# Attention followed by a SwiGLU block on one core: the first block's third chunk is projected with the third block's in a wide group, the output weights are asked for later, the last visits are dealt anew

## The chip, the core and the metric

The kernel runs on one core of a Trainium2 chip. The core has a matrix engine (TensorE, PE in the profile; its weight loads are listed as PEld), a vector engine (VectorE, DVE), an activation engine (ScalarE, ACT), GpSimd (POOL) and a queue engine (SyncE, SP). TensorE writes its products into PSUM, here eight banks of 512 single-precision columns on 128 partitions. Vector and activation engine read them from there. Transfers between the chip's memory and the core's are issued by POOL and SP and carried out by 16 DMA engines that both share. The metric is the device time of one execution in microseconds; lower is better.

## The reference

Twelve heads of softmax attention over eight batches of 448 tokens, head size 64, then a gated feed-forward layer (768 to 1536 and back) over all 3584 tokens:

```python
scores = scale * np.matmul(q, k.transpose(0, 1, 3, 2))
attn = exp(scores - max) / sum
x = (attn @ v).transpose(0, 2, 1, 3).reshape(B * S, H * D)   # 3584 x 768
g = x @ w_gate                                              # 768 x 1536
silu = g * (1.0 / (1.0 + np.exp(-g)))
val = x @ w_val
out = silu * val @ w_out                                    # 1536 x 768
```

## The kernel before

**Attention in pairs, units and visits.** Two heads make a pair; there are 48 pairs, six to a batch. From pair 12 on (`QUAD`), the scores of two neighbouring pairs are made in seven units: three key chunks of each pair and one unit that holds the remaining keys of both (`RU`). A unit (`qk_quad`, L349 to L383) is a few matmuls into one PSUM tile of pool `ps_s` (three buffers of two banks), and one exponential of 128 x 896 on ACT (L378) into SBUF. When all units of a pair are there, 32 or 40 small matmuls (L462, "PV" below) multiply the exponentials with the values. They write into two tiles `acc`, one for each head, of pool `ps_f`, which has two buffers of one bank. DVE closes each tile with a reciprocal (L504) and a multiplication (L505).

The program is written out by hand as a row of visits, and each engine works its own instructions in the order of the program. A visit of the middle and late part starts three units, runs the PV of at most one pair whose units all belong to earlier visits (some visits have none), and then takes some feed-forward work. `VISITS` (L1100) deals that work to the visits from `base` on: a row says which block begins, how many gate-and-value steps run (`nf`), how many wide groups (`ng`), how many plain outputs (`no`), and how many vector sums (`ns`). Visits are numbered here from `base`, the row's index in `VISITS`; the ones before `base` have negative numbers, and there `run_budget` spreads the work over the visits by its time.

**Where operands come from.** POOL loads the pairs' queries, keys and values (L203, L180), the weights (`load_w`, L223) and copies each pair's queries and keys into an order that suits a transposing transfer (L240). SP issues this transfer (`qkT<-qk`, L244), and only then can the pair's units start. `wq` (L1043) says behind which pair the weights and some further loads are asked for. POOL works its loads and copies in program order, and every load goes through one queue.

**The feed-forward blocks.** Two batches make 896 tokens, cut into a block of 384 and one of 512 tokens. Blocks 0 to 3 (batches 0 to 3) run during attention, in 12 gate-and-value steps each, whose results stand in `hts`. The output projection is made for chunks of 128 tokens in two ways:

- Plain: `plain_out` (L724), 12 matmuls into one PSUM tile for 384 output columns (`OH`) or 192 (`QW`).
- In a wide group: `OutPair.wide` (L807) makes two chunks together by seven products of six 384-column matmuls (L759), a Strassen-like scheme, with sums of the chunks made beforehand on DVE (`h_sums`) and combinations on DVE and ACT between the products. It takes one `ps_s` tile and one `ps_f` tile.

Before the change the three chunks of block 0 and the third chunk of block 2 are plain, the first in six halves at visits -11 to -8 and the last in four quarters at visits 25, 26, 27 and 29. The five wide groups of this stage stand at visits 5, 8, 20, 28 and 31. `run_group` takes a list `behind` of units: for a visit with a group and no PV, the visit's three units are not started ahead of the group but two inside it and the third after it.

**After attention.** The last four batches are projected in `Unit`s (L897), again by seven products instead of eight, 448 columns wide. A unit's second PSUM bank is first written by ACT and then added to by matmuls. For the first two units of each half a matmul with the identity (`Z`, L964) writes that bank beforehand, so that later matmuls add to what ACT writes. Four such matmuls run in all. Outputs are collected in `osb` tiles of pool `fp` (four buffers) and stored by SP.

Of the kernel before, what the change touches and what calls it, by code (L numbers as in the profile page):

```python
# [10 lines left out]
FP32 = mybir.dt.float32  # L11
FP16 = mybir.dt.float16
# [5 lines left out]
NB = 2  # L18
# [3 lines left out]
LA = 6  # L22
# [43 lines left out]
def kernel(  # L66
# [87 lines left out]

    wo_all = consts.tile([128, 2, NFB, OH], FP16, name="wo")
    wo = [wo_all[:, i] for i in range(2)]
    qk16s = [consts.tile([128, 2, NC, 2, D], FP16, name=f"qk16_{i}") for i in range(3)]

    raw = {}
# [6 lines left out]
            nc.tensor.matmul(wp[:, 0 : w * 128], lhsT=warm[:], rhs=warm4[:, 0:w], start=True, stop=True)  # L166

    def load_qk32(pr):
        rq = fp.tile([P, 2, NC, D], FP32, tag="osb", bufs=4, name="rq")
        rk = fp.tile([P, 2, NC, D], FP32, tag="osb", bufs=4, name="rk")  # L170
        for dst, src in ((rq, q), (rk, k)):
            nc.sync.dma_start(dst[:], src[0, 2 * pr : 2 * pr + 2].rearrange("h (p c) d -> p h (c d)", c=NC))
        raw[pr] = (rq[:], rk[:])
# [570 lines left out]
            store(osb, kk, c0 + ch * 128, 128, 0, DM)  # L744

    def new_osb():
        return fp.tile([128, DM], FP32, tag="osb", bufs=4, name="osb")

    def ffn2_steps(kk, c0, hts, steps):
        osbs = {}  # L750
# [146 lines left out]
    class Unit:  # L897


        def __init__(self, u, w, x, tsum, hts):  # L900
            self.u, self.hts, self.w = u, hts, w
            self.kind = "gv"[u % 2]
            self.x, self.tsum = x, tsum
            self.g = ps_s.tile([128, 2, 512], FP32, tag="s", name="un")
            self.a, self.e = self.g[:, 0, 0:w], self.g[:, 1, 0:w]
            self.by = {"a": [], "e": []}
# [56 lines left out]

        def Z(self):  # L964
            self.bank()
            nc.tensor.matmul(self.b, lhsT=ident[:], rhs=self.xb(0, 0)[:, 0], start=True, stop=True)

        def A1(self):
            if self.u > 1:
# [48 lines left out]
    with tc.manual_schedule():  # L1018
# [6 lines left out]
        for vo in Vts:  # L1025
# [19 lines left out]
            1: [("V", 2), ("qk", 8, 1), ("g", 1), ("v", 1)],  # L1045
            3: [("qk", 9, 1), ("qk", 10), ("g", 2), ("v", 2)],
            4: [("g", 3), ("v", 3), ("qk", 12)],
            6: [("V", 3), ("o", 0)],
            8: [("o", 1)],
        }  # L1050

        def emit(item):
# [18 lines left out]
        def add_block(i, visits):  # L1071
            if i < B - 2 * NB:
                f1, own, n = block(i)
                fvq.extend(f1)
                kk, c0, hts = own
            else:
                own = None
            t_out = NFB * OH / 2400.0
            if i == 0:
                oq.extend([(ffn2_steps(*own, by_half(range(n // 128), OH)), t_out)] * (2 * (n // 128)))  # L1080
            if i < 2:
                if i:
                    ffn2_wait.append(own)
                    sums.extend(wsums)
                    wsums.clear()
                return
            kk, c0, hts = ffn2_wait.pop()
            ffn2_wait.append(own)
            odd = i % 2 == 0
            new = [OutPair(kk, c0, hts, t, 1 - t if i == B - 2 * NB else t) for t in range(1 + odd)]  # L1090
            groups.extend(new)
            if not odd:
                w = QW
                oq.extend([(ffn2_steps(kk, c0, hts, by_half([2], w)), t_out)] * (DM // w))
            for pair in new:
                pair.todo = pair.sums()
                sums.extend(pair.todo)
# [10 lines left out]
        ]  # L1108

        def token_sums(x, w, t, eng=nc.vector):  # L1110
# [61 lines left out]

        def run_group(units):
            pair = groups.pop(0)
            if units:
                sums.insert(0, lambda: None)
                sums.insert(1, tsums6.pop(0))
            assert not any(f in sums for f in pair.todo)
            keep = [fp.tile([128, 512], FP32, tag=tag, name=name) for tag, name in (("sg", "p1"), ("t1", "p15"))]
            pair.wide(keep, add_sum, (1, 1, 0), units[:2])  # L1180
            for unit in units[2:]:
                qk(*unit)
# [93 lines left out]
        for x, (chunks, todo) in enumerate(plan):  # L1276
# [12 lines left out]
            lone = nf == 1 and bool(todo)  # L1289
            behind = []  # L1290
            for n, (pr, c) in enumerate(ordered if x else []):
                if ng and not todo:
                    behind.append((pr, c, small))
                    continue
                if n == 2 and ordered[n] in quads:
                    rests = open_products(rests, small)
                late = n == 2 and not todo and c < NC and pr < QUAD and bool(fvq) and not fvq[0].at[1]
                late = late or n == 2 and lone and not fvq[0].at[1]
                qk(pr, c, small, late)
# [15 lines left out]
            for pr in entered:  # L1315
                lead = [pr + 3] if pr + 3 < QUAD else [pr + 3, pr + 4] if pr + 3 == QUAD else [pr + 4]
                for p in lead:
                    if NPE <= p < NPAIR and p not in QPE:
                        ready.append(prep(p))
                if 14 <= pr + LA < NPAIR:  # L1320
                    load_qk16(pr + LA, 1)
                if 12 <= pr + 3 < NPAIR:
                    load_v(pr + 3)
# [77 lines left out]
                tsums6.pop(0)()  # L1401
            for u in {len(VISITS) + base - 6: range(2), len(VISITS) + base - 2: range(2, 3)}.get(x, []):
                weight_sums(u)
            while held and not fvq:
                turn_x(held.pop(0))
            while turns:
# [52 lines left out]

        def units_of(kk, t, last):  # L1460
            units = {}
            items = unit_items(units, lambda u: Unit(u, S, X[kk], t, hts), S)
            pairs = [OutPair(kk, 0, hts, p, p % 2, last and p == 2) for p in range(3)]
            if last:
                mixed = OutPair(kk, 0, hts, 0, 1)
                mixed.x, mixed.y = apart_chunk, hts[:, :, ts(6, 128)]
                mixed.rows = [(kk - 1, 6 * 128), (kk, 6 * 128)]
                pairs.insert(1, mixed)
                pairs[2].at = 2
            for n in range(NH):  # L1470
                after = [f"G{n - 1}"] if n else [f"F00_{NH - 1}", f"F10_{NH - 1}", f"D1_{NFB - 1}"]
                items[f"G{n}"] = (PE_, OH / 2400 + 0.0025, after, lambda n=n: pairs[0].begin(n))
            items["H0"] = (DVE_, 0.65, [f"F00_{NH - 1}", f"F10_{NH - 1}"], pairs[0].sums()[0])
            for part, f0, n, u in (("e", 0, 4, NFB - 3), ("l", 4, 2, NFB - 1)):
                for m, fn in enumerate(pairs[0].sums(f0, n)[1:], 1):
                    after = [f"F00_{u}", f"F10_{u}", "H0"] + [f"H{m - 1}{part}"] * (m > 1)
                    items[f"H{m}{part}"] = (DVE_, 0.07 + 0.1 * n, after, fn)
            return items, pairs
# [70 lines left out]
```

## Time and profile before

| | |
|---|---|
| median of three runs | 419.72 us (419.65 to 419.94) |
| the profiled execution's own time | 420.16 us |
| its span, first to last instruction | 418.4 us |
| mean granted TensorE clock | 1.000 |
| PE busy | 412.3 us, 4346 matmuls |
| DVE busy | 271.1 us |
| ACT busy | 248.9 us |
| POOL busy | 227.5 us |

Times within the span are given from its start. A row of the timeline has start, duration, engine, line, operation, tile, shape and count, and in brackets how long the engine was idle before and what ended that. A duration of several merged matmuls includes the last one's way through the array, so neighbouring rows overlap; the distance from start to start is what a row takes of the engine. A row of the windows view has the stretch, its length, each engine's busy time with its count of instructions, the granted clock, the busy share of the DMA engines (several transfers at once can take it over 1) and what they moved in GB/s.

### The profile page before, as it was taken

The numbers are of one execution on the slowest core, as the hardware profiler recorded it, in microseconds if no ns is written. First come the engines' busy times: TensorE is split into PE (matmuls) and PEld (weight loads), VectorE is DVE, ScalarE is ACT, GpSimd is POOL, SyncE is SP. The second block draws the span as 40 slices with busy tenths as digits, with TensorE's granted clock in tenths as the row PEclk, the third lists the DMA queues.
The fourth block names the chain that finished last, engine by engine and source line by source line (L and its number), as shares of the span: only waits on it lengthen the run. The fifth ranks groups of instructions, "written<-read, shape, count | busy, mean of one in ns | idle before, by whom it ended". The sixth has DMA issues, their size and how long they took to land.

```text
span 418.4 us, 10870 instructions
## 1 busy us (share of the span) xinstructions
PE 412.3 (99%) x4346; PEld 260.6 (62%) x4346; DVE 271.1 (65%) x630; ACT 248.9 (59%) x387; POOL 227.5 (54%) x346
## 2 busy tenths in 40 slices
PE   8999999999999999999999999999999999999996
PEld 3666666555577776787767676555555555555654
DVE  4767562566786774677756577765757665757763
ACT  6985676666577665787657686655453345454121
POOL 8856533999998983599977815599700000000000
PEclk9999999999999999999999999999999999999999
DMA  8999999999999999999999944600000430000225
GB/s 135 180 199 200 200 177 195 137 169 206 197 167 140 151 207 146 183 153 160 157 153 183 107 59 105 190 14 0 2 0 2 129 99 0 2 0 0 76 80 149
DMA packets 108196, 50.29 MB, mean 120 GB/s; under 512 B 60401, under 2 KB 104817, under 8 KB 108145
## 3 DMA queue, kind: packets, MB, share of 16 engines
q0 software_dynamic: 46848, 24.56, 51.4%
q1 hardware_dynamic: 61024, 24.79, 32.9%
q8 instruction: 34, 0.56, 0.6%
q10 hardware_dynamic: 272, 0.25, 0.2%
q14 instruction: 18, 0.14, 0.1%
HBM read 49.55 MB, written 11.01 MB: 145 GB/s over the span
## 4 chain that ended last, share of the span: by engine, by line
PE 81%; DMA 13%; POOL 4%; issue 1%; ACT 0%; DVE 0%; POOLq 0%
PE un L929 13%; PE gp L610 11%; PE og L759 11%; PE ub L929 10%; PE vp L610 9%; PE acc L462 9%; PE ob L759 8%; PE s L356 5%; DMA wv<-in_moe_w_val_dram 5%; DMA qkraw<-in_q_dram 4%; DMA wg<-in_moe_w_gate_dram 2%; DMA qkT<-qk 2%; PE op L732 2%; POOL qkraw L203 2%; PE s L368 1%
## 5 line engine op out<-in xcount | busy, mean ns | idle before, releaser
L378 ACT ACTIVATE E<-s 128x896 f16<-128x896 f32 x126 | 107.4, 916 | 37.5 <-PE s L356 27.4
L610 PE MATMUL gp<-X,wg 128*128 128x256 f16 (+3 forms) x402 | 61.7, 300 | 0.0
L610 PE MATMUL vp<-X,wv 128*128 128x256 f16 (+3 forms) x402 | 58.6, 289 | 0.0
L240 POOL COPY qk<-qkraw 128x512 f16<-128x512 f16 x70 | 44.8, 681 | 22.8 <-DMA qkT<-qk 21.9
L610 PEld LDWEIGHTS <-wv 128*128 128x128 f16 x444 | 41.7, 98 | 14.5
L180 POOL DMA_DIRECT2D vraw<-in_v_dram x72 | 43.8, 624 | 11.4 <-DMA wo<-in_moe_w_out_dram 7.6
L180 POOL DMA_DIRECT2D qkraw<-in_k_dram x70 | 42.3, 616 | 6.9 <-DMA wo<-in_moe_w_out_dram 3.9
L610 PEld LDWEIGHTS <-wg 128*128 128x128 f16 x402 | 35.5, 98 | 15.8 <-issue 2.2
L403 ACT ACTIVATE E<-s 112x896 f16<-112x896 f32 x48 | 40.7, 918 | 7.5 <-PE s L393 7.5
L462 PEld LDWEIGHTS <-E 128*128 128x128 f16 (+2 forms) x1224 | 38.1, 98 | 8.4 <-issue 3.1
L462 PE MATMUL acc<-vo,E 128*128 128x65 f16 (+2 forms) x1224 | 42.0, 193 | 0.1
L759 PEld LDWEIGHTS <-hts 128*128 128x128 f16 x282 | 27.1, 98 | 17.0
L690 DVE SCALAR_TENSOR_TENSOR t<-sg,gp 128x384 f32<-128x384 f32 (+1 forms) x29 | 17.4, 614 | 25.6 <-ACT sg L637 25.6
L696 DVE SCALAR_TENSOR_TENSOR hts<-t,vp 128x256 f16<-128x256 f32 (+3 forms) x67 | 30.9, 461 | 3.4 <-PE vp L610 1.2
L505 DVE TENSOR_TENSOR xt<-acc,R 128x256 f16<-128x256 f32 x72 | 30.6, 425 | 2.5
L203 POOL DMA_DIRECT2D qkraw<-in_q_dram x44 | 29.9, 679 | 3.2 <-PE tp L324 1.0
L356 PE MATMUL s<-qkT 64*64 64x448 f16 (+1 forms) x288 | 28.7, 352 | 0.3 <-DMA qkT<-qk 0.3
L994 ACT ACTIVATE silu<-un 128x448 f32<-128x448 f32 x24 | 13.1, 544 | 21.7 <-PE un L929 21.1
L759 PE MATMUL og<-wo,hts 128*128 128x384 f16 x132 | 25.4, 326 | 0.0
L978 DVE TENSOR_TENSOR un<-ub,kept 128x448 f32<-128x448 f32 x24 | 15.1, 630 | 15.5 <-ACT kept L975 9.8
L982 DVE TENSOR_TENSOR kept<-ub,kept 128x448 f32<-128x448 f32 x24 | 15.0, 625 | 13.3 <-PE ub L929 13.3
L971 ACT ACTIVATE ub<-un 128x448 f32<-128x448 f32 x24 | 12.7, 529 | 15.5 <-PE un L929 13.9
(213 smaller groups left out, 746.6 us busy)
## 6 DMA issues: line engine op xcount, KB each, us to landing
vraw<-in_v_dram POOLq DMA_DIRECT2D x72, 64.0 KB, 5.2
qkraw<-in_q_dram POOLq DMA_DIRECT2D x41, 112.0 KB, 4.8
qkraw<-in_k_dram POOLq DMA_DIRECT2D x68, 64.0 KB, 4.9
out_dram<-osb SPq DMA_DIRECT2D x7, 336.0 KB, 3.2
wg<-in_moe_w_gate_dram POOLq DMA_DIRECT2D x8, 288.0 KB, 9.4
wv<-in_moe_w_val_dram POOLq DMA_DIRECT2D x8, 288.0 KB, 10.0
wo<-in_moe_w_out_dram POOLq DMA_DIRECT2D x2, 1152.0 KB, 18.8
out_dram<-osb SPq DMA_DIRECT2D x7, 288.0 KB, 3.7
```

What stands on the lines that cost most here:

```text
L180: eng.dma_start(dst[ts(s, 64)], rows)
L203: nc.gpsimd.dma_start(dst, flat.rearrange("h (p c) d -> p h (c d)", c=NC))
L240: nc.gpsimd.tensor_copy(dst.rearrange("p c h d -> p h c d"), src)
L356: nc.tensor.matmul(s[ts(half, m), hx, 0:S].rearrange("p (c q) -> p c q", q=P), lhsT=t[ts(hx, 64), ds((c + low(pr, hx)) * 128 + half * m, m ...
L378: nc.scalar.activation(e, s[:, :, 0:S], AF.Exp, scale=sm_scale)
L403: nc.scalar.activation(e[:, :, 0:S], s[0:P, :, 0:S], AF.Exp, scale=sm_scale)
L462: nc.tensor.matmul(acc[ds(lo, m), ts((j + pr % 2) % (KR + 1), D + 1)], lhsT=e[rows, ds(hx * S + j * 128 + lo, m)], rhs=Vts[pr % NV][rows, ...
L505: nc.vector.tensor_tensor(xt[:, :, hx], a4[:, :, 0:D], r[:].unsqueeze(2).to_broadcast([128, KR + 1, D]), ALU.mult,)
L610: nc.tensor.matmul(dst[:, 0:w], lhsT=wslice(kind, self.fb, cb), rhs=X[kk][:, cb, ds(c0 + lo, w)], start=(cb == 0), stop=(cb == NCB - 1),)
L696: nc.vector.scalar_tensor_tensor(self.hts[:, self.fb, ds(lo, w)], self.t1[:, ds(lo, w)], 0.5 * HS, vp[:, 0:w], ALU.mult, ALU.mult)
L759: nc.tensor.matmul(dst, lhsT=lhs(n), rhs=rhs(n), start=first and n == 0, stop=n == NH - 1, skip_group_check=True)
L929: mm = nc.tensor.matmul(dst, lhsT=lhs[:, n], rhs=rhs[:, n], start=first and n == 0, stop=n == NK - 1, skip_group_check=True,)
```

## The change

Block 0's third chunk is no longer projected plainly. Two DVE copies at x = 14 and 16 (visits -5 and -3) keep its 128 tokens in a new tile `first_single`. When block 3 is added, a group `mixed` is built of that chunk and block 2's third chunk, which replaces the four quarters. So six plain halves become four, four plain quarters go, and there are six wide groups instead of five. `osb` gives up one of its four buffers, which makes room for `first_single`.

`wq` asks for the two halves of `w_out` behind pairs 8 and 9 instead of 6 and 8, and pair 15's queries and keys behind the second half. POOL's order around it becomes: third group of values, pair 11's copies, pair 14's load, first half of `w_out`, pair 13's copies, pair 12's values, second half of `w_out`, pair 15's load, pair 14's copies. Before, the first half of `w_out` stood ahead of pair 11's copies, the second ahead of pair 13's, and pair 12's values behind pair 15's load.

The last visits are dealt anew: visit 24 has one gate-and-value step and visit 25 the last one (before: two at visit 24, none at 25). The wide groups stand at 20, 27, 29 and 31, and nothing but attention stands at 26, 28, 30 and 32. For a group in a visit behind such an empty one, the visit's units now also go into and behind the group where the visit has a PV. PE's order from visit 25 on is then, with U for a unit: 3 U, PV 40, a step in halves | 3 U, PV 41 | PV 42, group with 2 U inside, 1 U | 3 U, PV 43 | PV 44, group with 2 U inside, 1 U | 3 U, PV 45 | group with 2 U inside, 1 U | 1 U, PV 46, PV 47. Before it was: 3 U, PV 40, quarter | 3 U, PV 41, quarter | 3 U, PV 42, quarter | 3 U, PV 43, group | 3 U, PV 44, quarter | 3 U, PV 45 | group with 2 U inside, 1 U | 1 U, PV 46, PV 47.

`Z` writes only the columns that no earlier matmul has written into that bank: 188 of 448 in the first half, 64 in the second, without clearing.

```diff
+    first_single = consts.tile([128, NFB, 128], FP16, name="single")
...
-        rq = fp.tile([P, 2, NC, D], FP32, tag="osb", bufs=4, name="rq")
+        rq = fp.tile([P, 2, NC, D], FP32, tag="osb", bufs=3, name="rq")
...
         def Z(self):
             self.bank()
-            nc.tensor.matmul(self.b, lhsT=ident[:], rhs=self.xb(0, 0)[:, 0], start=True, stop=True)
+            lo = self.primed
+            nc.tensor.matmul(
+                self.b[:, lo:],
+                lhsT=ident[:],
+                rhs=self.xb(0, 0)[:, 0, lo:],
+                start=False,
+                stop=True,
+                skip_group_check=True,
+            )
...
-            6: [("V", 3), ("o", 0)],
-            8: [("o", 1)],
+            6: [("V", 3)],
+            8: [("o", 0)],
+            9: [("o", 1), ("qk", 15, 1)],
...
-                oq.extend([(ffn2_steps(*own, by_half(range(n // 128), OH)), t_out)] * (2 * (n // 128)))
+                oq.extend([(ffn2_steps(*own, by_half(range(2), OH)), t_out)] * 4)
...
-            new = [OutPair(kk, c0, hts, t, 1 - t if i == B - 2 * NB else t) for t in range(1 + odd)]
+            new = [OutPair(kk, c0, hts, t) for t in range(1 + odd)]
             groups.extend(new)
             if not odd:
-                w = QW
-                oq.extend([(ffn2_steps(kk, c0, hts, by_half([2], w)), t_out)] * (DM // w))
+                mixed = OutPair(kk, c0, hts, 0, 1)
+                mixed.x, mixed.y = first_single, hts[:, :, ts(2, 128)]
+                mixed.rows = [(0, 2 * 128), (kk, c0 + 2 * 128)]
+                new.append(mixed)
+                groups.append(mixed)
...
-            (0, 0, 1, 0, 0), (0, 1, 0, 0, 0), (0, 1, 0, 0, 0), (0, 1, 0, 0, 0), (0, 2, 0, 0, 0),
-            (4, 0, 0, 1, 1), (0, 0, 0, 1, 1), (0, 0, 0, 1, 2), (0, 0, 1, 0, 0), (0, 0, 0, 1, 2),
-            (0, 0, 0, 0, 0), (0, 0, 1, 0, 0), (0, 0, 0, 0, 0),
+            (0, 0, 1, 0, 0), (0, 1, 0, 0, 0), (0, 1, 0, 0, 0), (0, 1, 0, 0, 0), (0, 1, 0, 0, 0),
+            (0, 1, 0, 0, 0), (4, 0, 0, 0, 1), (0, 0, 1, 0, 1), (0, 0, 0, 0, 2), (0, 0, 1, 0, 1),
+            (0, 0, 0, 0, 2), (0, 0, 1, 0, 0), (0, 0, 0, 0, 0),
...
         def run_group(units):
             pair = groups.pop(0)
-            if units:
+            if units and not groups:
                 sums.insert(0, lambda: None)
                 sums.insert(1, tsums6.pop(0))
...
-                if ng and not todo:
+                if ng and (not todo or not any(VISITS[x - base - 1][1:4])):
                     behind.append((pr, c, small))
                     continue
...
-                if 14 <= pr + LA < NPAIR:
+                if 14 <= pr + LA < NPAIR and pr + LA != 15:
                     load_qk16(pr + LA, 1)
...
+            if x in (14, 16):
+                part = ds((x - 14) // 2 * NH, NH)
+                nc.vector.tensor_copy(first_single[:, part], hview(0, 384)[:, part, ts(2, 128)])
```

More of the change, by code (lines that the diff above doesn't have):

```diff
@@ L746, in new_osb @@
     def new_osb():
-        return fp.tile([128, DM], FP32, tag="osb", bufs=4, name="osb")
+        return fp.tile([128, DM], FP32, tag="osb", bufs=3, name="osb")
     def ffn2_steps(kk, c0, hts, steps):
@@ L897, with __init__ @@
     class Unit:
[L900 to L901 removed]
+        def __init__(self, u, w, x, tsum, hts, primed):
+            self.u, self.hts, self.w, self.primed = u, hts, w, primed
             self.kind = "gv"[u % 2]
@@ L1461, in units_of @@
             units = {}
-            items = unit_items(units, lambda u: Unit(u, S, X[kk], t, hts), S)
+            items = unit_items(units, lambda u: Unit(u, S, X[kk], t, hts, OH if last else (KR + 1) * (D + 1)), S)
             pairs = [OutPair(kk, 0, hts, p, p % 2, last and p == 2) for p in range(3)]
```

2 lines of the change are left out of this document (1 added, 1 removed).

## The prediction

> **What bounds the kernel now.** I read the page first, then TensorE's waits, then the stages that the change touches: windows, timeline, POOL's queue.
>
> ```profile
> span 418.4 us, 10870 instructions
> PE 412.3 (99%) x4346; PEld 260.6 (62%) x4346; DVE 271.1 (65%) x630; ACT 248.9 (59%) x387; POOL 227.5 (54%) x346
> DMA  8999999999999999999999944600000430000225
> PE s L356 <- DMA qkT<-qk: 0.3, 1, 0.3
> ```
>
> PE is the bound, and its longest wait for data is 0.3 us (last line, from the waits by engine). So every matmul removed is time won, unless it lets PE run into something that it now just misses. The DMA row shows a candidate: the DMA engines are full until the 23rd slice.
>
> The last visits of attention, by windows: visits 24 and 25; 26 and 27; 28; 29 and 30; 31; the end up to the first `Unit`.
>
> ```profile
> 232.71:241.32 8.61, 8.61 (x93) 5.25 (x92) 4.94 (x13) 5.84 (x8) 7.24 (x11) 1.00 0.80 96
> 241.32:248.58 7.26, 7.26 (x168) 5.81 (x167) 5.73 (x18) 6.89 (x10) 0.76 (x1) 1.00 0.26 51
> 248.58:255.50 6.92, 6.92 (x48) 4.01 (x46) 3.67 (x10) 2.70 (x5) 2.14 (x2) 1.00 0.68 91
> 255.50:259.93 4.43, 4.43 (x90) 3.36 (x90) 4.10 (x11) 3.75 (x5) 1.96 (x3) 1.00 0.43 86
> 259.93:267.45 7.52, 7.52 (x56) 4.07 (x52) 4.95 (x10) 4.41 (x7) 4.35 (x5) 1.00 0.74 190
> 267.45:270.22 2.77, 2.75 (x71) 2.12 (x71) 2.51 (x7) 2.25 (x3) 1.42 (x2) 1.00 0.76 217
> sum 37.51, PE 37.49 PEld 24.62 DVE 25.90 ACT 25.84 POOL 17.88; mean PE 6.25 PEld 4.10 DVE 4.32 ACT 4.31 POOL 2.98
> ```
>
> In visits 26 and 27 ACT (fourth busy column, 6.89 of 7.26 us) is nearly as full as PE: the exponentials are close to being the bound there, and a quarter of plain output is what PE does meanwhile. A group without units takes 6.92 us, one with two units inside 7.52.
>
> **The last visits.** The change takes the four quarters out and puts a sixth group in. What it also does is to set PV 41 against PV 42 and PV 43 against PV 44 with nothing between. Each PV takes both `ps_f` banks.
>
> ```profile
> 244.82 1.14 PE L462 MATMUL acc<-vo,E 64*128 64x65 f16 x32
> 245.80 1.15 PE L732 MATMUL op<-wo,hts 128*128 128x192 f16 x12
> 246.40 0.42 DVE L505 TENSOR_TENSOR xt<-acc,R 128x256 f16<-128x256 f32 x1
> 246.88 0.38 PE L368 MATMUL s<-qkT 64*64 64x448 f16 x4
> 255.50 0.74 PE L356 MATMUL s<-qkT 64*128 64x448 f16 x6
> 255.96 2.54 ACT L378 ACTIVATE E<-s 128x896 f16<-128x896 f32 x3 [0.84 <-PE s L356]
> 256.08 1.25 PE L462 MATMUL acc<-vo,E 64*128 64x65 f16 x32
> 256.28 0.85 DVE L1114 TENSOR_TENSOR vraw<-X 128x1344 f16<-128x1344 f16 x1
> L378 ACT ACTIVATE E<-s 128x896 f16<-128x896 f32 x126 | 107.4, 916 | 37.5 <-PE s L356 27.4
> ```
>
> A PV holds PE for 0.98 us (244.82 to 245.80), but DVE has read its second bank only at 246.82 (246.40 + 0.42), 2.0 us after the PV began. Before, the quarter (1.08 us, 245.80 to 246.88) and the next units filled that time. Now PE waits: 2.0 + 0.05 - 1.0 = 1.05 us, twice. Behind the waiting PV stand, on PE, its own matmuls and the whole group.
>
> The second wait is for `ps_s`. Behind the groups at 27 and 29 stand one unit and then the next visit's three: four units in a row with three tiles, so the fourth waits for the first's exponential. Three units take PE 0.58 us (255.50 to 256.08); an exponential starts 0.46 us behind its unit (255.96) and takes 0.916. So the fourth starts at 0.46 + 0.92 + 0.03 = 1.4 us instead of 0.6: 0.8 us, at visits 28 and 30. These units' exponentials follow at (2.54 - 0.92) / 2 = 0.81 us and end 3.8 us behind the group; PV 44 wants the last at about 4.0, so ACT doesn't add to it.
>
> Stretch by stretch, from the same point as the windows:
> - Visits 24 and 25: the same two steps, less one quarter: 8.61 - 1.08 = 7.5 us.
> - 26 and 27: units 0.58, PV 41 to PV 42 2.05, PV 42 1.0, group with two units of 0.19 and their change of shape 7.4: 11.0.
> - 28 and 29: units 1.6, PV 43 to PV 44 2.05, PV 44 1.0, group 7.4: 12.05.
> - 30: units 1.6, PV 45 1.0: 2.6. Then 7.52 + 2.77 = 10.3 as before.
>
> Together 43.5 us against 37.51: **+6.0**. Without the four waits (2 x 1.05 + 2 x 0.8 = 3.7) it would be +2.3, the lower bound; the upper is one us more, if DVE's sums, which now stand between the closes of the two PVs (the largest 0.85 us, 256.28), also come late.
>
> ```profile
> 238.80 2.48 SPq L550 DMA_TRANSPOSE X<-xt  x2
> 241.33 1.23 SPq L556 DMA_TRANSPOSE X<-xt  x1
> ```
>
> On SP, the transposes of pairs 36 to 40, held until the last step is done, now start at visit 25's end. PV 42's closing needs the third of them gone (issued 2.5 us behind the first). That close comes 3.5 us into visit 26, so DVE may stand there for an estimated 1 to 2 us; but PE needs the bank next for the group's third product, two products (6.92 / 7 each) and two units behind PV 42, 2.4 us. I count nothing.
>
> **The first block.** Four plain halves instead of six.
>
> ```profile
> L732 PE MATMUL op<-wo,hts x72: 323/326/337, 64.8 to 81.8; 128*128 128x384 f16 x72
> 48.80 16.49 DMA qkraw<-in_q_dram
> 56.26 0.59 POOL L180 DMA_DIRECT2D qkraw<-in_k_dram  x1 [0.74 <-DMA vraw<-in_v_dram]
> 64.44 0.59 POOL L180 DMA_DIRECT2D vraw<-in_v_dram  x1 [7.59 <-DMA wo<-in_moe_w_out_dram]
> 72.44 0.59 POOL L180 DMA_DIRECT2D qkraw<-in_k_dram  x1 [3.92 <-DMA wo<-in_moe_w_out_dram]
> 67.36 9.11 DMA qkT<-qk
> 74.56 1.18 POOL L240 COPY qk<-qkraw 128x512 f16<-128x512 f16 x2
> L244 SPq DMA_TRANSPOSE qkT<-qk x1: 1232/1232/1232, 75.8 to 75.8; - x1
> DMA to landing us min/median/max: 6.4/6.4/6.4
> 76.51 0.36 PE L356 MATMUL s<-qkT 64*128 64x448 f16 x2 [0.34 <-DMA qkT<-qk]
> 78.07 4.08 PE L732 MATMUL op<-wo,hts 128*128 128x384 f16 x24
> 82.85 0.38 PE L368 MATMUL s<-qkT 64*64 64x448 f16 x4
> wo<-in_moe_w_out_dram POOLq DMA_DIRECT2D x2, 1152.0 KB, 18.8
> vraw<-in_v_dram POOLq DMA_DIRECT2D x72, 64.0 KB, 5.2
> 55.97:64.16 8.19, 8.17 (x121) 5.42 (x118) 5.90 (x14) 5.78 (x9) 0.59 (x1) 1.00 1.37 171
> 64.16:72.16 8.00, 8.00 (x85) 4.79 (x81) 1.72 (x5) 5.61 (x9) 3.54 (x6) 1.00 1.35 199
> ```
>
> 24 matmuls in 4.0 us (78.07 to 82.08, where the next units start): two halves less are -3.9 us, and the wait at 76.51 (0.4 with its restart) can go, since pair 14 is now loaded ahead of the weights. PE would then want pair 15 (L368, the unit that it shares with pair 14) at 82.85 - 4.3 = 78.5. But this stretch has a second clock. POOL's queue lands its loads one behind the other; POOL's waits show when: values at 56.2, half of `w_out` at 64.4, pair 14's queries at 65.3 (48.80 + 16.49), its keys some 0.7 later, the other half at 72.4, pair 15 before 74.56. Then come the copies (1.18 us), the transpose (75.8 + 6.4 = 82.2), and the unit at 82.85: PE has 0.6 us to spare. The change alters the order in that queue but takes no byte out ahead of pair 15; it puts pair 12's values (two loads of 64 KB) there too, 0.7 us at the second half's pace (1152 KB from 66.0 to 72.4, 180 KB/us). So pair 15 is turned at 74.56 + 0.7 + 1.18 + 6.4 = 82.9, and the unit stands at 83.0: **+0.2** instead of -4.3. On its way PE meets the second half of `w_out` first: the third plain half comes at about 71.4 (the first at 64.8 and 1.0 for the next visit's units, that now stand ahead of it, then two halves and one visit's units and PV, 3.9 + 1.6), the weights at 72.4 + 0.7 = 73.1; that wait is part of the same 4.5 us.
>
> Bounds: -4.3 if neither is late. Above, +1.8 more: the second half may go at the first's pace (56.2 to 64.4, 8.2 us instead of 6.4), since pair 14's transpose (67.36, 9.11 us), which ran beside it for 5 us, is now asked for earlier and may run beside it throughout. I take +0.2, nearest the landings.
>
> The Trainium skill (DMA: Bandwidth & Descriptors, "Queues, rings and completion order") says that a DMA engine takes packets from its queues by turns. The rows don't settle it: with a transpose beside it for 5 of its 6.4 us the second half was still the faster one. By that rule alone the upper bound is the likelier, and the sum 1.8 us higher.
>
> **The identity matmuls.**
>
> ```profile
> 270.79 0.35 PE L966 MATMUL ub<-X,ident 128*128 128x448 f16 x1
> 270.98 0.73 PE L929 MATMUL un<-vraw,qkraw 128*128 128x448 f16 x3
> ```
>
> One holds PE 0.19 us for 448 columns. With 188 and 64 columns in proportion, 0.08 and 0.03: 2 x 0.11 + 2 x 0.16 = **-0.5**.
>
> **At nothing.** The two copies into `first_single` and the mixed group's four sums lie on DVE, which is 65% busy; at no more than the 0.85 us of the larger sum above, the six would cost at most 5 us uncovered. Three `osb` buffers instead of four: a buffer is written again a whole group (6.9 us) after its store was asked for, so its store has that long.
>
> **The sum.** +6.0 + 0.2 - 0.5 = +5.7 us on the span of 418.4: 424.1, or 425.9 with the 1.76 us around it (420.16). The median of the runs is 0.44 below that execution: **425.4 us**.
>
> **The rivals.**
> - *Weights slower still* (+1.8 at the second half of `w_out`, above): 427.2. For it: the DMA engines' share of 1.35 to 1.37. Against: with 1.35 the second half went faster.
> - *The early gain arrives*: pair 15 comes by 78.5. Then 425.4 - 4.5 = 420.9. For it: POOL no longer stands 7.59 us behind `wo`. Against: its queue was never empty meanwhile.
> - *The late visits stay packed*, the early gain is lost: 425.4 - 3.7 = 421.7. For it: PE shows no such wait now. Against: both PVs use the only two `ps_f` banks.
> - *PE's own count decides*, the other side: with nothing late in either stage +2.3 - 0.5 - 4.3 = -2.5, 417.2. It becomes faster once pair 15 comes by 78.5 and the four late waits cost under 2.5 us together (6.0 - 3.7 + 2.5 = 4.8). For it: the 99%; against: both points above.
>
> **Numbers.** Forecast 0.57, weights slower 0.12, early gain 0.12, packed visits 0.10, PE's count 0.09. Range 420.8 to 427.8, which leaves out the last; the forecast's own is 423.5 to 426.8. About 0.2% (0.84 us) is what can be told from no change: faster 0.09, same 0.02 (between the last two), slower 0.89.
>
> **What would show it.** In the profile after: PE waits of about 1 us for DVE in the second of two adjoining PVs, twice, and of 0.8 us for ACT at the fourth unit; the stretch from visit 24 to the first `Unit` at 43.5 us; PE waiting for `wo` or `qkT` between 65 and 83 us, and L368 of pairs 14 and 15 no earlier than 82. If that unit comes near 78.5, the queue argument is wrong; if the adjoining PVs run without a gap, the bank argument is.

## The result and the profile after

The changed kernel takes **430.05 us** (median of five runs, 429.41 to 430.60) against 419.72 us before: a ratio of **1.0241, 95% interval 1.0230 to 1.0253**. The forecast was 425.4 us with a range of 420.8 to 427.8: slower, as said, but by 10.3 us instead of 5.7, and outside the range. The profiled span went from 418.4 to 428.1 us.

From the page of the changed kernel, the rows that answer to those of before:

```profile
span 428.1 us, 10843 instructions
PE 414.6 (97%) x4322; PEld 259.9 (61%) x4322; DVE 282.3 (66%) x638; ACT 249.6 (58%) x388; POOL 226.4 (53%) x346
PEclk9999989999999999999999999999999999999999
DMA  9999999999999999999999624330000250000225
```

PE is busy for 97% instead of 99%, and the clock row has an 8 in its sixth slice, where before no slice fell below 9. The waits of PE by what ended them (total, times, longest):

```profile
PE xtp L541 <- DVE xt L448: 3.1, 1, 3.1
PE s L357 <- ACT E L379: 1.2, 2, 0.7
PE ob L760 <- DVE xt L506: 1.2, 2, 0.8
...
PE acc L463 <- DVE hts L697: 0.6, 1, 0.6
PE acc L463 <- DVE xt L506: 0.5, 2, 0.3
PE acc L463 <- DVE R L505: 0.5, 1, 0.5
PE acc L463 <- ACT E L379: 0.5, 1, 0.5
```

Apart from 1.0 us for the warm-up at the start, which both kernels have and which is left out here, the longest before was 0.3 us. The first row is early; the others belong to the late visits. Here are those visits in the windows view of the changed kernel: visits 24 and 25; 26 and 27 with the unit behind the group; 28 and 29; 30; the end up to the first `Unit` (length, then busy time of PE, PEld, DVE, ACT and POOL, clock, DMA share, GB/s):

```profile
233.90:242.62 8.72, 7.99 (x87) 4.89 (x87) 4.82 (x13) 6.33 (x9) 7.79 (x11) 1.00 0.75 102
242.62:254.66 12.04, 10.47 (x132) 6.43 (x132) 6.61 (x17) 5.74 (x8) 1.98 (x3) 1.00 0.28 57
254.66:267.16 12.50, 10.93 (x133) 6.53 (x133) 9.19 (x20) 6.54 (x9) 2.48 (x2) 1.00 0.48 114
267.16:269.75 2.59, 1.90 (x41) 1.33 (x41) 0.72 (x2) 2.12 (x3) 0.18 (x1) 1.00 0.68 165
269.75:280.05 10.30, 10.29 (x127) 6.20 (x124) 7.47 (x17) 6.64 (x10) 5.78 (x7) 1.00 0.37 108
sum 46.15, PE 41.57 PEld 25.37 DVE 28.81 ACT 27.37 POOL 18.20; mean PE 8.31 PEld 5.07 DVE 5.76 ACT 5.47 POOL 3.64
```

46.15 us against 37.51: **+8.64**. PE's busy time grew by 4.1 us (37.49 to 41.57), its idle time from 0.02 to 4.58. The place of each wait is in the timeline of the changed kernel, in the brackets at the end of the rows:

```profile
238.96 1.11 PE L463 MATMUL acc<-vo,E 64*128 64x65 f16 x31 [0.61 <-DVE hts L697]
...
244.82 0.19 PE L463 MATMUL acc<-vo,E 64*128 64x65 f16 x1 [0.46 <-ACT E L379]
245.28 1.13 PE L463 MATMUL acc<-vo,E 64*128 64x65 f16 x31 [0.27 <-DVE xt L506]
...
249.68 1.15 PE L760 MATMUL ob<-E,hsum 128*128 128x384 f16 x6 [0.84 <-DVE xt L506]
...
256.03 0.38 PE L357 MATMUL s<-qkT 64*64 64x448 f16 x4 [0.51 <-ACT E L379]
...
268.59 0.37 PE L357 MATMUL s<-qkT 64*128 64x448 f16 x2 [0.69 <-ACT E L379]
```

In their order: PV 40 waits for the gate-and-value step of visit 24; PV 42 waits twice behind PV 41 (PV 44 does the same at 257.84); the third product of the group at visit 27 waits for DVE (that of visit 29 too, 0.32 us at 262.18); the fourth units at visits 28 and 30 wait for an exponential.

The whole account of the 9.74 us by which the span grew, each from the start of one marker to the next:

| stretch | forecast | measured |
|---|---|---|
| start to the unit of pairs 14 and 15 (82.85, now 83.61) | +0.2 | +0.76 |
| from there to visit 24 (232.71, now 233.90) | 0 | +0.43 |
| visit 24 to the first `Unit` | +6.0 | +8.64 |
| first `Unit` to the end (270.22 to 418.38, now 280.05 to 428.12) | -0.5 | -0.09 |

### The profile page after: what moved, and what is told of

The parts are those of the page before. It is cut to its first block, busy times and chain, and to the rows that moved or that the text cites. A ratio compares the mean times of both kernels' runs of the same rounds, so it can differ in the third digit from the quotient of the medians.

```text
span 428.1 us, 10843 instructions
## 1 busy us (share of the span) xinstructions
PE 414.6 (97%) x4322; PEld 259.9 (61%) x4322; DVE 282.3 (66%) x638; ACT 249.6 (58%) x388; POOL 226.4 (53%) x346
## 4 chain that ended last, share of the span: by engine, by line
PE 86%; DMA 4%; DVE 4%; ACT 2%; issue 1%; SPq 1%; DVEq 0%; ACTq 0%
PE gp L611 12%; PE un L930 12%; PE og L760 11%; PE vp L611 10%; PE ub L930 9%; PE ob L760 9%; PE acc L463 7%; PE s L357 5%; DMA vraw<-in_v_dram 3%; PE s L394 2%; PE acc L427 2%; PE op L733 2%; ACT E L379 1%; PE s L369 1%; PE wp L167 1%
## 5 line engine op out<-in xcount | busy, mean ns | idle before, releaser
L760 PEld LDWEIGHTS <-hts 128*128 128x128 f16 x294 | 28.2, 98 | 18.2 <-DVE hts L595 0.5
L760 PE MATMUL ob<-E,hsum 128*128 128x384 f16 (+1 forms) x126 | 22.0, 311 | 1.2 <-DVE xt L506 1.2
```

What stands on the lines that cost most here:

```text
L760: nc.tensor.matmul(dst, lhsT=lhs(n), rhs=rhs(n), start=first and n == 0, stop=n == NH - 1, skip_group_check=True)
```

## The experiments

All kernels in one table. Ratios are to the kernel before, run on the same chip; "unit" is the start of the unit that pairs 14 and 15 share, "late" the stretch from visit 24 to the first `Unit`, both from the profiled execution, in us. In `values_first` and `pool_24` only the unit's first matmul stands there; the other three wait for pair 15 until 85.02 and 83.86.

| kernel | median | ratio, 95% interval | unit | late |
|---|---|---|---|---|
| before | 419.72 | | 82.85 | 37.51 |
| the change | 430.05 | 1.0230 to 1.0253 | 83.61 | 46.15 |
| early_only | 421.80 | 1.0029 to 1.0064 | 85.03 | 37.51 |
| late_only | 428.45 | 1.0188 to 1.0223 | 82.70 | 45.96 |
| z_osb_only | 420.09 | 0.9994 to 1.0017 | 82.50 | 37.47 |
| values_first | 430.67 | 1.0246 to 1.0277 | 83.28 | 45.90 |
| copied_half_after | 426.14 | 1.0137 to 1.0168 | 80.12 | 46.25 |
| copied_half_before | 420.29 | 1.0000 to 1.0019 | 82.80 | 37.51 |
| weights_later | 428.90 | 1.0184 to 1.0222 | 78.43 | 46.23 |
| one_ahead | 427.75 | 1.0167 to 1.0201 | 83.54 | 43.69 |
| other_pool | 432.57 | 1.0290 to 1.0325 | 84.17 | 48.03 |
| steps_at_24 | 428.89 | 1.0195 to 1.0230 | 83.16 | 45.11 |
| pool_24 | 428.30 | 1.0146 to 1.0221 | 82.62 | 44.39 |
| weights_later_one_24 | 426.87 | 1.0147 to 1.0182 | 78.11 | 43.92 |
| no_quarters | 418.97 | 0.9967 to 0.9987 | 82.53 | 36.45 |

### The parts alone

`early_only` (the kernel before with the early edits):

```diff
-                oq.extend([(ffn2_steps(*own, by_half(range(n // 128), OH)), t_out)] * (2 * (n // 128)))
+                oq.extend([(ffn2_steps(*own, by_half(range(2), OH)), t_out)] * 4)
...
-            6: [("V", 3), ("o", 0)],
-            8: [("o", 1)],
+            6: [("V", 3)],
+            8: [("o", 0)],
+            9: [("o", 1), ("qk", 15, 1)],
```

> The kernel before with the early part of the change alone: four plain halves in the first block instead of six and the new order of the loads; the third chunk of the first block (128 tokens of the output) is left out, and the late visits, the Unit stage and the four output buffers stay as they were. Theory A, the early gain is lost in the first 84 us to the loads' own clock: the unit that pairs 14 and 15 share stands at 83.6 us as in the changed kernel (82.85 before), with PE's wait of about 3 us for a pair's closing near 55 us, and the end comes 0.5 to 1.3 us later than before: 420.2 to 421.0 us. Rival B, the early part wins and the late part costs more than its stretch shows: the two halves less arrive, the unit stands at 78.5 us and the time is 415.4 to 416.5 us. Rival C, the early part costs several us further on: above 422 us.

`late_only` (the changed kernel with these lines and `load_qk16`'s condition put back; the third chunk's plain rows are not stored):

> The changed kernel with the early part put back: six plain halves and the old order of the loads (the first block's third chunk is projected there too, without being stored, and again in the mixed group). Theory A, the two parts add up: the shared unit stands at 82.9 us again, the late stretch from visit 24 to the first Unit is 46.1 us as in the changed kernel, and the time is 428.7 to 429.5 us, so the late part carries 8.6 to 9.4 of the 10.3 us. Rival B, the late waits came from what the early part shifted: below 427.5 us. Rival C, the early part alone carries more than its own 0.8 to 2 us: also below 427.5 us.

`z_osb_only` (the kernel before with the edits of `Z` and of `osb`):

> The kernel before with the narrower identity matmuls and three output buffers instead of four, nothing else. Theory A, the Unit stage is held by a chain that the identity matmuls are no part of, as the unchanged 144.1 us of that stage in both kernels suggest, and the buffers are free in time: 419.5 to 420.0 us, no change. Rival B, the matmuls gain their 0.5 us and something else of the change took it back: 419.2 us. Rival C, the third buffer comes late somewhere: above 420.4 us.

The parts add up: +0.29 to +0.64% for the early one, +1.88 to +2.23% for the late one, nothing for the third, +2.30 to +2.53% together. The early part is a loss by itself, and a larger one than theory A allowed (421.80 us against at most 421.0): PE's wait was 3.9 us in the profiled execution, the slowest of its eight runs. Rival B, that two plain halves less are time won, is out. `late_only` lies 0.25 us under theory A's range, far above the rivals' 427.5, and has no wait near 55 us. The narrower identity matmuls bring nothing: from the first `Unit` to the end it is 148.16 us before and 148.20 with them. The first two do start the matmuls behind them 0.22 us earlier, but 17 us on PE runs into a wait that it didn't have before, and is level again:

```profile
289.87 0.73 PE L929 MATMUL ub<-qkraw,E 128*128 128x448 f16 x3 [0.15 <-DVE un L986]
```

### Where the early gain went

In the changed kernel PE stands near 55 us, which the prediction did not foresee. Rows of its timeline:

```profile
56.63 0.62 DVE L222 COPY vo<-vraw 112x512 f16<-112x512 f16 x1 [2.57 <-DMA vraw<-in_v_dram]
57.39 0.62 DVE L448 TENSOR_TENSOR xt<-acc,R 128x448 f16<-128x448 f32 x1
58.07 0.41 PE L541 MATMUL xtp<-ident,xt 128*128 128x128 f16 x3 [3.06 <-DVE xt L448]
```

DVE cannot copy a pair's values before the third group of values has landed, the closing of the pair ahead stands behind that copy, and PE needs the closing for a transpose. The kernel before had PE at the same PV 1.6 us later (55.45 against 53.87) and a whole gate-and-value step between it and the transpose; there DVE's copy waited for the values as well, but only 0.35 us and until 55.99. From the timeline of before:

```profile
55.45 0.35 PE L426 MATMUL acc<-vo,E 112*128 112x65 f16 x6
...
56.42 1.14 PE L610 MATMUL gp<-X,wg 128*128 128x384 f16 x6
```

`run_budget` gives each visit its share of the work that is left, and with two plain halves less it no longer puts a gate-and-value step into this visit. `values_first` moves the values ahead:

```diff
-            4: [("g", 3), ("v", 3), ("qk", 12)],
-            6: [("V", 3)],
+            4: [("g", 3), ("qk", 12)],
+            6: [("V", 3), ("v", 3)],
```

> The changed kernel with one pair of loads moved in POOL's queue: the last quarter of the value weights stands behind the third group of values instead of ahead of pair 12's loads. Theory A, in the changed kernel PE stands 3.1 us near 55 us because DVE cannot close a pair before that group of values lands at 56.6 us, and then runs 3.4 us at half the granted clock: here the values land 2 to 4 us earlier, the wait falls under 1 us, no record shows a clock of 0.5 there, and the unit of pairs 14 and 15 moves from 83.6 us to 82.0 to 82.3 us, not further, because pair 15 is turned only at 81.6 us: 428.4 to 429.0 us against 430.05. Rival B, all of the lost 4.8 us returns: 425.5 us. Rival C, the order of the queue doesn't matter, since the next wait (the weights or pair 12) takes the place: 429.8 to 430.5 us.

PE's waits in it:

```profile
PE op L733 <- DMA wo<-in_moe_w_out_dram: 3.4, 1, 3.4
PE s L369 <- DMA qkT<-qk: 1.4, 1, 1.4
PE xtp L541 <- DVE xt L448: 1.0, 1, 1.0
```

The wait shrank to 1.0 us and the clock stayed whole in the profiled execution, yet nothing was won: the time moved to the weights and to pair 15. Rival C comes nearest (430.67 us, just above its range). The next two kernels take the second load of output weights out of the queue and copy it on the chip instead, in this kernel and in the kernel before:

```diff
+            if i:
+                return
             src = moe_w_out[:, ts(i, OH)].rearrange("(f p) m -> p f m", p=128)
...
+            if x == 9:
+                nc.vector.tensor_copy(wo[1], wo[0])
```

> The kernel with the values ahead (values_first), in which the second half of the output weights is no longer loaded but copied by DVE from the first half at visit -10, so 1152 KB less go through POOL's queue ahead of pair 15; the output's columns from 384 on are made with the wrong weights. Theory A, the loads' own clock sets the pace up to 84 us: the wait of 3.4 us for the weights and that of 1.4 us for pair 15 go, the shared unit moves from 84.9 us to 80.0 to 80.8 us, and the end comes 4 to 5 us earlier than in values_first: 425.6 to 426.7 us. Rival B, PE or its partners have no more to give there (another wait takes the place): 429.5 to 430.9 us.

> The kernel before with the same copy in place of the second load of output weights (columns from 384 on are made with the wrong weights). Theory A, with six plain halves PE needs these 84 us itself, its only wait there is 0.4 us, so the 1152 KB less bring no more than that: the shared unit at 82.2 to 82.9 us, 419.4 to 420.2 us beside 420.1. Rival B, the loads set the pace of the kernel before as well: 2 us or more faster, under 418.2 us.

Both came as theory A said: the unit at 80.12 us and 426.14 us in all against 430.67, and no gain in the kernel before (420.29 us, against 419.94 on the same chip). So with six plain halves PE hardly waits for the loads (0.3 us in all); with four, the loads set the pace, and the two halves are worth nothing as long as these loads are in the queue.

`weights_later` asks for that half three pairs later and puts its two plain halves behind it:

```diff
-            9: [("o", 1), ("qk", 15, 1)],
+            9: [("qk", 15, 1)],
+            12: [("o", 1)],
...
+                if x in (14, 16):
+                    oq.append(second.pop(0))
+                    out_small[0] = True
+                    run_o()
+                    out_small[0] = False
```

> The kernel with the values ahead (values_first), in which the second half of the output weights is asked for three pairs later, behind pair 15 and its successors, and the two plain halves that need it, with the weights' sums, go to visits -5 and -3. Nothing is left out. Theory A, up to 84 us the loads set the pace, and behind that they have room: without 1152 KB and without two halves (3.9 us) ahead of it the unit of pairs 14 and 15 comes at 76 to 78.5 us, the halves then cost PE their 4 us later, and the time is 425.6 to 427 us against 430.67 for values_first, as with the copied half (426.14). Rival B, the loads have no room behind 84 us either: a wait for the weights or for a later pair takes the 4 us back, 429.5 us or more.

It hit neither forecast: the unit came at 78.43 us, but visit 24 starts at 232.96 against 233.90 in the changed kernel, so 4.2 of the 5.2 us were given back, 3.9 of them by the two halves that had only moved. My 425.6 us had counted them as won.

### Where the late time went

`one_ahead` puts a unit between the two PVs:

```diff
-                if ng and (not todo or not any(VISITS[x - base - 1][1:4])):
+                if ng and (not todo or n > 0 and not any(VISITS[x - base - 1][1:4])):
```

> The changed kernel with one unit of visits 27 and 29 set between the two PVs, ahead of the group, instead of behind the group. Theory A, the late visits lose 1.5 us to the fourth unit in a row behind each group (0.7 and 0.86 us) and 1.7 us to the two adjoining PVs (0.87 us each): the first two waits go, the second two shrink by a unit's 0.2 us each, and the stretch from visit 24 to the first Unit goes from 46.15 to 44.2 us or so, 427.9 to 428.4 us in all. Rival B, exponentials set the pace of these visits: the unit between the PVs or the group then waits for its tile instead, and the time stays at 429.6 to 430.4 us. Rival C, the wait of the group for the late closing (X transposes) grows by what is won here: no change either, but with that wait at 1.5 us or more each.

As theory A said: the late waits for exponentials are gone from PE's list, and the stretch lost 2.46 us (46.15 to 43.69), 0.5 us more than expected. The group's waits for DVE fell from 1.2 to 0.5 us as well.

`other_pool` opens PV 42 and PV 44 in a `ps_s` tile (`pv_open(p0, True)` in `open_products` for these two):

> The changed kernel with PV 42 and PV 44 written into one ps_s tile each instead of the two ps_f tiles that the PV ahead of them holds. Theory A, the 0.87 us that PE stands at each of these PVs come from the closing of the PV ahead: both go, the stretch from visit 24 to the first Unit goes from 46.15 to 44.4 us, 428.2 to 428.6 us in all. Rival B, the third tile is missed by the units and the group: the waits for exponentials grow by as much, 429.6 to 430.5 us. Rival C, something else holds PE there (exponentials late for the PV): the gaps inside the PV stay, 430 us.

Slower: the third tile is missed, as rival B had it, but by far more than it allowed. The timeline of `other_pool`:

```profile
248.90 0.42 DVE L506 TENSOR_TENSOR xt<-acc,R 128x256 f16<-128x256 f32 x1 [2.83 <-DMA X<-xt]
249.93 0.36 PE L357 MATMUL s<-qkT 64*128 64x448 f16 x2 [2.09 <-DVE xt L506]
```

No PE row inside PV 42 waits any more (PV 41 and PV 42 take 2.12 us together instead of 3.03), so the bank was the cause there; in PV 44 0.5 us is left, for an exponential that comes nearly as late as the bank did. But DVE closes PV 42 late, since the close overwrites an `xt` whose transpose has not gone, and the tile is missed meanwhile. Behind this pause PE then ran for 3.4 us, from 251.0 on, at half the granted clock, as a window out of that time shows (length, PE's busy time, clock, DMA share, GB/s):

```profile
251.50:254.00 2.50, 2.50 (x10) 0.50 0.28 56
```

That cost about 1.7 us, an estimate from 3.4 us at 0.50. Without it the stretch (48.03 us against 46.15) would be about as long as in the changed kernel, as rival B said. The same wait of DVE stands in the changed kernel, in the timelines of SP and of DVE:

```profile
242.72 2.48 SPq L551 DMA_TRANSPOSE X<-xt  x2
245.25 1.23 SPq L557 DMA_TRANSPOSE X<-xt  x1
246.57 3.19 SPq L551 DMA_TRANSPOSE X<-xt  x2
249.19 0.42 DVE L506 TENSOR_TENSOR xt<-acc,R 128x256 f16<-128x256 f32 x1 [2.94 <-DMA X<-xt]
```

`steps_at_24` lets these transposes go a visit earlier, by putting both last steps at visit 24:

```diff
-            (0, 0, 1, 0, 0), (0, 1, 0, 0, 0), (0, 1, 0, 0, 0), (0, 1, 0, 0, 0), (0, 1, 0, 0, 0),
-            (0, 1, 0, 0, 0), (4, 0, 0, 0, 1), (0, 0, 1, 0, 1), (0, 0, 0, 0, 2), (0, 0, 1, 0, 1),
+            (0, 0, 1, 0, 0), (0, 1, 0, 0, 0), (0, 1, 0, 0, 0), (0, 1, 0, 0, 0), (0, 2, 0, 0, 0),
+            (0, 0, 0, 0, 0), (4, 0, 0, 0, 1), (0, 0, 1, 0, 1), (0, 0, 0, 0, 2), (0, 0, 1, 0, 1),
```

> The changed kernel with the last two gate-and-value steps together at visit 24, as before the change, and nothing but attention at visit 25. Theory A, the waits of the group at 27 and 29 for the late closing (0.9 and 0.3 us) come from the transposes that are held until the last step and so start a visit later, and the wait inside PV 40 (0.96 us) from the step at visit 24: all three go; against that PV 40 and PV 41 stand three units apart without work between them (about 1.5 us for exponentials and the bank): 429.0 to 430.0 us, a small gain, with no wait of DVE for X transposes over 1 us near 249. Rival B, the waits for the late closing have another cause and stay: 431 us or more.

DVE's wait for `X<-xt` is gone and so is the wait of PV 40; the stretch is 1.04 us shorter. Of the group's two waits for the late closing the first is gone, but not the second, at visit 29:

```profile
PE ob L760 <- DVE xt L506: 0.3, 1, 0.3
```

So theory A's cause holds for the first alone. PE's waits for exponentials rose from 1.2 us to 1.8. `pool_24` is both edits together:

> steps_at_24 with PV 42 and PV 44 in one ps_s tile each, as in other_pool, which was slower because such a tile stayed taken until DVE closed it, 2.9 us late for the X transposes. Theory A, with the transposes a visit earlier the tile is closed in time: the two waits of 0.87 us at the adjoining PVs are gone and nothing takes their place, 1.2 to 1.8 us faster than steps_at_24. Rival B, the third tile is missed in any case: not faster than steps_at_24.

Its runs spread too far to tell its time from that of `steps_at_24` (425.6 to 429.3 us). By its stretch it is 0.72 us shorter than `steps_at_24`, half of what theory A expected.

`no_quarters` asks what the four quarters were worth in the kernel before (its `oq.extend` for the third block and the four `no` entries of `VISITS` removed):

> The kernel before without the four plain quarters of visits 25, 26, 27 and 29; the third chunk of the third block (128 tokens of the output) is left out, nothing takes its place. They hold PE 4 x 1.08 = 4.3 us. Theory A, most of that filled waits: without them the visits have two PVs and six units in a row, exponentials and the closing of the PV ahead then hold PE, and only 1.5 to 2.5 us are won: 417.8 to 418.8 us beside 420.2. So the group that replaced them pays its whole 6.9 us and wins little back. Rival B, PE's count decides there too: all 4.3 us are won, 415.6 to 416.3 us, and the late loss in the changed kernel is the new waits alone.

0.9 us, less than either theory gave: in the stretch 1.06 of the 4.3 us that they hold PE. Rows of its timeline show where most of the rest went (PE's waits for exponentials come to 1.9 us):

```profile
241.36 0.38 PE L356 MATMUL s<-qkT 64*64 64x448 f16 x4 [0.43 <-ACT E L378]
243.79 0.36 PE L356 MATMUL s<-qkT 64*128 64x448 f16 x2 [0.45 <-ACT E L378]
246.22 0.38 PE L356 MATMUL s<-qkT 64*64 64x448 f16 x4 [0.43 <-ACT E L378]
...
239.59 9.01 ACT L378 ACTIVATE E<-s 128x896 f16<-128x896 f32 x11
```

Eleven exponentials run without a gap for 9 us. Where no feed-forward work stands between the units, ACT sets the pace and PE waits at each visit's third unit.

Last, `weights_later_one_24` joins `weights_later`, `one_ahead` and `steps_at_24`:

> weights_later with one unit between the two PVs at visits 27 and 29 and both last steps at visit 24: what pays of the three experiments put together. If they add up: 426.3 less 2.3 less 0 to 1, 423.0 to 424.3 us; if the parts share a wait, 425 us or more. The kernel before (420.1 us) is beaten only if the late stretch falls from 46.15 to under 40 us.

The parts share their waits: 426.87 us, and its late stretch is no shorter than that of `one_ahead` alone (43.92 against 43.69). No version of the change that was tried beats the kernel before.

## Why the prediction was right and wrong

**The direction was right, and so was the argument on the loads; the early time was met by another wait.** The unit of pairs 14 and 15 came at 83.61 us, near the forecast's 83.0 and not at 78.5, and the copied half shows that the loads hold PE there once the wait near 55 us has shrunk. But the sign that the prediction named, PE waiting for `wo` or `qkT` between 65 and 83 us, is not in the changed kernel; it stands in `values_first` (3.4 and 1.4 us). That the unit came within 0.6 us of its forecast is therefore partly luck. The prediction let the visits up to the first plain half stand as they were, "the first at 64.8". It came at 70.86, because a step had moved behind the PV near 55 us and PE stood 3.1 us for values there.

The wait had a second price, a lower clock, of about 1.7 us (an estimate, from 3.4 us at 0.50). The granted clock in the windows view of the changed kernel, across that wait and behind it:

```profile
54.80:58.00 3.20, 0.21 (x7) 0.08 (x3) 1.33 (x3) 1.33 (x2) 3.16 (x6) 1.00 1.37 187
60.00:61.50 1.50, 1.50 (x31) 1.36 (x28) 0.72 (x2) 1.50 (x2) 0.90 (x2) 0.50 1.26 189
63.00:65.00 2.00, 2.00 (x14) 1.22 (x13) 1.19 (x3) 0.49 (x1) 0.00 (x0) 1.00 1.37 101
```

**The late stretch had the right mechanisms and four terms missing or mis-sized.** The four waits came as forecast. From the start of PV 41 to the group's took 3.03 us and from PV 43 to the group's 3.04, against 2.05 + 1.0; the four units at visits 28 and 30 took 1.56 and 1.62 us against 1.6. (The 0.87 us for an adjoining PV in the expectations is a little low: in `other_pool`, without the wait, the two PVs took 0.91 us less.) Visit 30 and the end (2.59 and 10.30) fell on their forecasts. The 2.7 us over the forecast's sum lie in the other three stretches:

- Visits 24 and 25, 8.72 instead of 7.5. The step that failed is "the same two steps, less one quarter". One step alone in a visit without a PV ends on DVE when PV 40 already wants its bank (0.61 us of idle). From the units of visit 25 to the end of PV 40 it took 2.62 us (237.29 to 239.91) instead of 1.54 (238.70 to 240.24). Before, two interleaved steps stood there, and with both at visit 24 again (`steps_at_24`) the wait is gone.
- Visits 26 and 27, 12.04 instead of 11.0. The step that failed is "I count nothing" for the held transposes. The prediction saw the late close and gave DVE 1 to 2 us; it stood 2.94, PE was there 2.6 us behind PV 42, and 0.84 were paid. `steps_at_24` shows the cause.
- Visits 28 and 29, 12.50 instead of 12.05. Here 0.32 us were paid for DVE's sums between the closes, which the prediction had only in its upper bound, "the largest 0.85". Two of them took 1.15 and 1.56 us, and the close came behind them (rows of the changed kernel):

```profile
258.94 1.15 DVE L595 TENSOR_TENSOR hts<-hts 128x768 f16<-128x768 f16 x1
260.01 1.56 DVE L1127 TENSOR_TENSOR vraw<-X 128x1344 f16<-128x1344 f16 x1
262.18 1.15 PE L760 MATMUL ob<-E,hsum 128*128 128x384 f16 x6 [0.32 <-DVE xt L506]
```

- In both of these stretches the group took 7.58 us beside its wait instead of 7.4, 0.36 us together. The forecast's own row for a group with two units has 7.52.
- Beneath all of them, the quarters were counted as 4.3 us won and 3.7 us of new waits set against that. `no_quarters` shows that 3.3 of the 4.3 us were cover even before. The sum allowed for much of it by the waits, but it speaks against the rival "PE's count decides" as well: with the quarters left out and nothing in their place, PE's count fell by 4.3 us and the time by 0.9.

**The identity matmuls** were counted as -0.5 us because PE was busy; they brought nothing (`z_osb_only`), since another wait takes up what the first two save. Three `osb` buffers and DVE's two copies at no cost were right. DVE's sums at no cost were not: beside the 0.32 us at visit 29, 0.39 of the +0.43 us between the first block and visit 24 are one late start of `vp`, behind a sum that is shown at the end.

**The chances.** The early gain and the packed visits, 0.22 together, were both refuted, and so was "weights slower still" as a cause: the second half of `w_out` landed at about 74.0 us (asked for at 56.08, 17.9 us to landing), 0.9 us later than forecast, but PE, late itself, did not wait for it. The range failed because the late stretch's upper bound held one us for DVE's sums and nothing else: the 2.94 us that DVE stood for the transposes, the wait of PV 40 and the wait near 55 us were in no bound.

## What to carry to other kernels

Work of the bounding engine is worth removing only where that engine alone sets the pace: here 3.9 us beside loads were worth nothing, and 4.3 us between exponentials were worth 1. Ask of each piece that is removed what waited behind it, best by a run that leaves it out with nothing in its place. And where a scheduler spreads work by what is left, removing a piece moves others; follow the order up to the first wait ahead of the edit too.

## What the hardware showed

- **The clock falls behind a pause, but not behind each.** PE's idle 3.1 us near 55 us in the changed kernel were followed by some 3.4 us at a granted clock of 0.50 (the windows above). In `early_only` (3.9 us idle) and in `other_pool` (2.7 us idle at the same place) it lasted about twice as long, until 64 and 63 us. Later in `other_pool` a pause of 2.1 us (247.84 to 249.93) was enough for 3.4 us at 0.50, which began at 251.0, when PE had been at work again for 1.1 us (its window stands with that experiment). A row of each one's windows view near 60 us, with PE alone, and the wait of the second:

```profile
62.00:64.00 2.00, 2.00 (x22) 0.50 1.80 162
```

```profile
58.50:61.00 2.50, 2.50 (x43) 0.50 1.27 191
```

```profile
PE xtp L541 <- DVE xt L448: 2.7, 1, 2.7
```

In the profiled execution of `values_first`, with 3.4 us idle ahead of 76.20 us, the clock stayed whole. The Trainium skill (TensorE: Matmul & The Clock Gate, "Part 1: The HAM clock gate") gives a free-running window of 3.4 us and says that an idle one halves the clock. That a drop lasts one window or two and that a pause may slip between two windows agrees with these rows; that the pause has to fill a window does not, since 2.1 us were enough.
- **DVE's sums stretch beside POOL's work.** A sum of 0.68 us in the kernel before took 1.68 us in the changed one, where it started within 0.04 us of a POOL copy. In the timelines of after and of before:

```profile
153.53 1.29 POOL L241 COPY qk<-qkraw 128x512 f16<-128x512 f16 x2
153.57 1.68 DVE L596 TENSOR_TENSOR hsum<-hts 128x768 f16<-128x768 f16 x1
```

```profile
151.87 1.21 POOL L240 COPY qk<-qkraw 128x512 f16<-128x512 f16 x2
152.82 0.68 DVE L595 TENSOR_TENSOR hsum<-hts 128x768 f16<-128x768 f16 x1
```

The closings behind it came late and PE's `vp` waited. The two sums that delayed the group at visit 29 also began inside a POOL operation of the changed kernel:

```profile
258.38 1.30 POOL L896 TENSOR_TENSOR qk<-wv,qk 128x384 f16<-128x384 f16 x1 [13.70 <-DMA qkT<-qk]
259.64 1.22 POOL L893 TENSOR_TENSOR qk<-wg 128x384 f16<-128x384 f16 x1
```

The Trainium skill (SBUF — State Buffer, "SBUF: two separate sides") says that such operations of DVE and POOL take a shared pair of ports in turn, one blocking the other. The rows agree with that. With POOL idle the sums take 0.55 us (at 247.46 in the kernel before) and 0.85 us (at 256.28 there), and all four, the 0.68, 1.68, 1.15 and 1.56 us, end 0.12 to 0.14 us before POOL's end plus that time. No run here moved the POOL operations away to show it.
